# Two of six lower parts by an accumulating transfer in place of a GpSimd subtraction (attention and gated layer, one core)

## The chip, the cores and the metric

One core of a Trainium2 chip runs the whole program. The metric is the device time of one execution in microseconds (us), the median of several runs. A separate profiled execution gives the trace.

## What is computed

`x` has shape 4 x 12480 x 128 and `inducing` 32 x 128; `w_in` is 128 x 2048, `w_out` 2048 x 128. For each of the four batches, with `s = 1/sqrt(128)`:

```
mab(q, kv) = softmax(s * q @ kv.T) @ kv
h = mab(inducing, x)           # 32 x 128: summary of the batch
y = mab(x, h)                  # 12480 x 128
u = y @ w_in                   # 12480 x 2048
g = u        where u >= 1
    0        where u <= -1
    (u+1)^2/4  between
out = g @ w_out                # 12480 x 128
```

## The kernel before, in words

The tokens of a batch stand in 26 chunks of 480, 104 chunks in all. Per batch, `summarize` makes `h` and multiplies it with `w_in` (tile `hw`, held as an upper and a lower fp32r part); `attend` makes the softmax weights of four chunks at a time (tile `aT`). Then `chunk` does the wide layer for 480 tokens. This part fills most of the time.

`chunk` walks over 8 pairs `k` of 128 hidden features each (NP = 8, 256 features a pair). For each pair: two hidden matmuls on TensorE into two PSUM banks (L953, "h"); on ScalarE `max(u+1, 0)` from PSUM into the tile `w` (L961, "r", one instruction for both banks where these lie side by side, 128 x 960, else two of 128 x 480), then the square over four (L947, "s"); on VectorE the bound, `min(max(u, 1), w)` (L966, "t"), which makes `w` the gated value `g`. The product with `w_out` is accumulated in one PSUM bank over all pairs (L1053), read as 8 pairs of two 128-feature halves, then transposed on VectorE (L1065, tile `oT`) and stored.

An fp32 matmul (tile `w` with weight `w_f`, pairs 2 and 5, "pf") takes TensorE much longer than an fp32r one. So six of the eight pairs (`SPLIT = (0, 1, 3, 4, 6, 7)`; the last chunk uses `END`) are split: an upper part `hi` of fp32r ("hi": on VectorE at L1024, ScalarE at L1021 or GpSimd at L1019, as the planner chooses), and a lower part `lo = w - hi` by a subtraction on GpSimd (L1027, "lo"). With the weight's own parts `w_hi` and `w_lo` there are three fp32r matmuls for each half: `w_lo` x `hi` and `w_hi` x `hi` ("p"), and `w_hi` x `lo` ("pl").

The order is set before anything runs. Every operation goes to a planner (`Plan`) with its engine or choice of engines, a cost, a lag until its result can be used, and a due time from the table `DUE` (ns, by kind and pair). `Plan.order` walks through planned time, takes for each engine the operation that is due first among those that are ready, assigns the buffers (`SLOTS`: 8 for `w`, 4 for `hi`, 4 for `lo`, 7 PSUM banks for the hidden values) and fixes the order in which each engine gets its instructions. Each engine's queue then runs strictly in that order and waits by semaphores. DMAs are issued on SyncE (SP), two each on ScalarE at the start and the end, and none on GpSimd.

`load_out` loads a pair's part of `w_out` (8-byte floats), joins it to fp32 and makes `w_f` or `w_hi` and `w_lo` once, during the first 62 us.

Of the kernel before, what the change touches and what calls it, by code (L numbers as in the profile page):

```python
# [9 lines left out]
F32 = mybir.dt.float32  # L10
F32R = mybir.dt.float32r
# [9 lines left out]

KEPT = {}

SLOTS = dict(
    h=7, o=1, xn=9, xT=26, xr=2, e1=1, eN=1, hw=6, hx=1, hy=1, w=8, hi=4, lo=4, aT=3, s2=2, a=1, ahi=1, oT=1
)
# [4 lines left out]


DUE = {
# [17 lines left out]
    "end": [-102350],  # L51
# [15 lines left out]
}  # L67

WARM = (28000, 180)
# [57 lines left out]
class Plan:  # L127
# [125 lines left out]
def attn_moe(  # L253
# [68 lines left out]
    def in_turn(pool, near=None):  # L322
        turns[pool] += 1
        return Slot(pool, turns[pool] - 1, near)
# [126 lines left out]
        joined = add(dict(DVE=(both, both + 130, due), POOL=(700, 850, due)), 0, 0, 0, join, [v], [mag, top])  # L451
        return joined, mag

    w_hi, w_lo, w_f, w_made = {}, {}, {}, {}
    in_made = []

    def load_in(j, when, due):
# [4 lines left out]
    def load_out(k, when, due):  # L462
        src = w_out[k * WS : (k + 1) * WS].rearrange("(p t) d -> p t d", t=2)
        whole, parted = any(k not in t for t in [SPLIT, END]), any(k in t for t in [SPLIT, END])
        by = lambda a: a.rearrange("p (t c) -> p t c", t=2)
        made, f = load_f32(src, when, due, after=got_all[0, 21])
        w_made[k] = []
        if whole:
            w_f[k] = const.tile([P, 2, C], F32, name=f"w_f{k}")
            w_made[k].append(add("ACT", 320, 450, due, lambda: nc.scalar.copy(w_f[k], by(f.tile)), [made], [f]))  # L470
        if not parted:
            return
        w_hi[k] = const.tile([P, 2, C], F32R, name=f"w_hi{k}")
        w_lo[k] = const.tile([P, 2, C], F32R, name=f"w_lo{k}")

        def lower():
            nc.gpsimd.tensor_sub(w_lo[k], by(f.tile), w_hi[k].bitcast(F32))

        made = add("ACT", 320, 450, due, lambda: nc.scalar.copy(w_hi[k], by(f.tile)), [made], [f])
        w_made[k].append(add("POOL", 650, 750, due, lower, [made], [f]))  # L480


    xT, xT_made, hT, hT_made, hw, hw_made = {}, {}, {}, {}, {}, {}
# [448 lines left out]
    def chunk(b, c):  # L932
# [4 lines left out]
        for k in range(NP):  # L937
# [39 lines left out]
            for i, h in enumerate(hs_):  # L977
                ts.append(add("DVE", 568, 700, at(due, "t", k) + i, ms[i], [s], [h, w]))
            plan.twins(*ts, 1070, 1200, LONE["t"])
            if kept:  # L980
                hi, lo = in_turn("hi"), in_turn("lo")
                for i, h in enumerate(hs_):
# [28 lines left out]
                    ([(w_hi, lo)], 218, "pl", ls, [lo]),  # L1011
                ]
            elif split:
                hi, lo = in_turn("hi"), in_turn("lo")

                def upper(hi=hi, w=w, by=[]):
                    engine = by[0].engine
                    if engine == "POOL":
                        nc.gpsimd.tensor_scalar(make(hi), w.tile, 1.0, 0.0, op0=ALU.mult, op1=ALU.add)  # L1019
                    elif engine == "ACT":  # L1020
                        nc.scalar.copy(make(hi), w.tile)  # L1021
                    else:

                        nc.vector.tensor_reduce(make(hi), w.tile.unsqueeze(3), axis=AX.X, op=ALU.max)  # L1024

                def lower(w=w, hi=hi, lo=lo):
                    nc.gpsimd.tensor_sub(make(lo), w.tile, hi.tile.bitcast(F32))  # L1027

                by = []
                ways = dict(  # L1030
                    DVE=(1061, 1285, at(due, "hi DVE", k)), ACT=(886, 1065, at(due, "hi ACT", k)),
                    POOL=(1000, 1180, at(due, "hi POOL", k)),
                )
                u = add(ways, 0, 0, 0, lambda upper=upper, by=by: upper(by=by), ts, [hi, w])
                by.append(u)
                l = add("POOL", 2236, 2340, at(due, "lo", k), lower, [u], [lo, w, hi])

                parts = [
                    ([(w_lo, hi), (w_hi, hi)], 436, "p", [u], [hi]),
                    ([(w_hi, lo)], 218, "pl", [l], [lo]),  # L1040
                ]
            else:
                parts = [([(w_f, w)], 806, "pf", ts, [w])]
            for terms, cost, kind, needs, uses in parts:
                for i in range(2):

                    def project(k=k, i=i, terms=terms):
                        for wt, g in terms:
                            first = acc.tile is None
                            if first:  # L1050
                                make(acc)
                            acc.parts -= 1
                            nc.tensor.matmul(  # L1053
                                acc.tile[:, :CW], wt[k][:, i, :], g.tile[:, i, :],
                                start=first, stop=(acc.parts == 0),
                            )

                    acc.parts += len(terms)
                    done.append(
                        add("PE", cost, cost + 200, at(due, kind, k) + i, project, [*needs, *w_made[k]], [*uses, acc])  # L1060
                    )


        def turn():
# [73 lines left out]
```

## Time and profile before

| what | before |
|---|---|
| median of 3 runs | 1733.42 us (1731.18 to 1733.91) |
| profiled execution: span | 1730.3 us |
| median less that span (what lies around the instructions, and the difference of executions) | 3.1 us |
| granted TensorE clock, mean | 0.999 |
| first output transpose / last | 93.9 us / 1725.1 us |
| HBM read / written | 48.94 MB / 25.56 MB |

The span goes from the first to the last instruction of the one profiled execution; its own time is the span and what lies around it, which the trace doesn't hold; the 3.1 us is the nearest to it that is known. PE is TensorE's matmuls, PEld its weight loads, DVE VectorE, ACT ScalarE, POOL GpSimd, SP the engine that issues DMAs. In a group's row stand line, engine, operation, what it writes and reads, the shapes and the count, then busy time in us and the mean length of one in ns, then the idle time of the engine just before them and what ended it. A row of waits gives a total in us, how many, and the longest.

### The profile page before, as it was taken

The numbers are of one execution on the slowest core, as the hardware profiler recorded it, in microseconds if no ns is written. First come the engines' busy times: TensorE is split into PE (matmuls) and PEld (weight loads), VectorE is DVE, ScalarE is ACT, GpSimd is POOL, SyncE is SP. The second block draws the span as 40 slices with busy tenths as digits, with TensorE's granted clock in tenths as the row PEclk, the third lists the DMA queues.
The fourth block names the chain that finished last, engine by engine and source line by source line (L and its number), as shares of the span: only waits on it lengthen the run. The fifth ranks groups of instructions, "written<-read, shape, count | busy, mean of one in ns | idle before, by whom it ended". The sixth has DMA issues, their size and how long they took to land.

```text
span 1730.3 us, 26049 instructions
## 1 busy us (share of the span) xinstructions
PE 1696.6 (98%) x8062; PEld 1229.5 (71%) x8062; DVE 1626.2 (94%) x2167; ACT 1664.2 (96%) x2486; POOL 1612.6 (93%) x875
## 2 busy tenths in 40 slices
PE   6999999999999999999999999999999999999998
PEld 5667777777767777777777777777777677777776
DVE  5799999999999999999999999999999999999997
ACT  5699999999999999999999999999999999999997
POOL 1599999999899999999999999999989999999997
PEclk9999999999999999999999999999999999999999
DMA  9443323333334233343143333232212111111111
GB/s 235 112 74 69 74 58 70 57 62 61 70 66 77 47 72 63 66 75 68 31 93 54 74 68 69 51 66 52 42 34 53 33 30 30 35 35 35 33 31 18
DMA packets 427950, 105.76 MB, mean 61 GB/s; under 512 B 370562, under 2 KB 421218, under 8 KB 427810
## 3 DMA queue, kind: packets, MB, share of 16 engines
q1 hardware_dynamic: 426722, 103.84, 30.5%
q8 instruction: 64, 1.05, 0.3%
q14 instruction: 76, 0.62, 0.1%
q10 hardware_dynamic: 1088, 0.25, 0.1%
HBM read 48.94 MB, written 25.56 MB: 43 GB/s over the span
## 4 chain that ended last, share of the span: by engine, by line
PE 62%; ACT 16%; DVE 11%; issue 5%; POOL 3%; DMA 2%; SPq 1%; DVEq 0%; ACTq 0%; POOLq 0%
PE banks L1053 43%; PE banks L953 14%; ACT w L961 8%; ACT w L947 6%; DVE w L966 6%; DVE hi L1024 3%; POOL lo L1027 2%; PE banks L611 1%; PE banks L765 1%; ACT hi L1021 1%; PE banks L554 1%; SPq L532 1%; DMA xr<-in_x 1%; DVE oT L1065 1%; PE banks L514 1%
## 5 line engine op out<-in xcount | busy, mean ns | idle before, releaser
L1027 POOL TENSOR_TENSOR lo<-w,hi 128x960 fp32r<-128x960 f32 x623 | 1395.9, 2271 | 40.3 <-DVE hi L1024 17.9
L966 DVE SCALAR_TENSOR_TENSOR w<-banks,w 128x480 f32<-128x480 f32 (+1 forms) x1200 | 960.6, 838 | 35.9 <-ACT w L947 30.7
L961 ACT ACTIVATE w<-banks 128x480 f32<-128x480 f32 (+1 forms) x1352 | 843.7, 700 | 15.0 <-PE banks L953 13.9
L947 ACT ACTIVATE w<-w 128x960 f32<-128x960 f32 x832 | 842.2, 1049 | 2.7
L953 PE MATMUL banks<-aT,hw 128*128 128x480 f32 x1664 | 605.6, 432 | 7.3 <-DVE w L966 5.2
L1053 PE MATMUL banks<-hi,w_lo 128*128 128x480 f32 x1246 | 492.0, 395 | 5.4 <-DVE oT L1065 3.3
L1024 DVE TENSOR_REDUCE hi<-w 128x960 fp32r<-128x960 f32 x409 | 464.7, 1142 | 18.2 <-PE banks L1053 1.2
L1053 PE MATMUL banks<-hi,w_hi 128*128 128x480 f32 x1246 | 472.9, 380 | 0.0
L953 PEld LDWEIGHTS banks<-aT,hw 128*128 128x128 f32 x1664 | 304.7, 188 | 167.6 <-DVE w L966 71.1
L1053 PE MATMUL banks<-w,w_f 128*128 128x480 f32 x836 | 391.4, 567 | 0.0
L1053 PE MATMUL banks<-lo,w_hi 128*128 128x480 f32 x1246 | 385.2, 395 | 0.8 <-POOL lo L1027 0.8
L1053 PEld LDWEIGHTS banks<-hi,w_lo 128*128 128x128 f32 x1246 | 234.2, 188 | 76.2 <-DVE oT L1065 18.0
L1053 PEld LDWEIGHTS banks<-lo,w_hi 128*128 128x128 f32 x1246 | 229.8, 188 | 76.2 <-POOL lo L1027 25.7
L1053 PEld LDWEIGHTS banks<-hi,w_hi 128*128 128x128 f32 x1246 | 234.2, 188 | 40.0 <-issue 7.2
L1053 PEld LDWEIGHTS banks<-w,w_f 128*128 128x128 f32 x836 | 155.9, 189 | 68.7 <-issue 50.9
L1019 POOL TENSOR_SCALAR hi<-w 128x960 fp32r<-128x960 f32 x140 | 139.6, 1002 | 19.3 <-DVE w L966 10.4
L1021 ACT CAST hi<-w 128x960 fp32r<-128x960 f32 x74 | 75.5, 1021 | 4.7 <-DVE w L966 3.1
L1065 DVE STREAM_TRANSPOSE oT<-banks 128x480 f32<-128x480 f32 x104 | 70.1, 674 | 7.9 <-PE banks L1053 6.5
L535 DVE STREAM_TRANSPOSE xT<-xr 128x480 f32<-128x480 f32 x78 | 51.2, 659 | 0.0
L808 POOL TENSOR_TENSOR a<-a,ahi 128x480 fp32r<-128x480 f32 (+1 forms) x28 | 34.5, 1232 | 0.6 <-ACT ahi L805 0.6
L441 POOL TENSOR_TENSOR w_in_sb<-hi,lo 128x256 f32<-128x256 f32 x8 | 6.1, 763 | 28.4 <-DVE hi L430 28.4
L611 PEld LDWEIGHTS banks<-xn,eN 120*32 120x32 f32 (+1 forms) x754 | 24.4, 109 | 11.1 <-ACT eN L603 4.4
(107 smaller groups left out, 580.0 us busy)
## 6 DMA issues: line engine op xcount, KB each, us to landing
out<-oT SPq DMA_DIRECT2D x414, 60.0 KB, 2.2
xn<-in_x SPq DMA_DIRECT2D x91, 240.0 KB, 4.2
xr<-in_x SPq DMA_DIRECT2D x312, 60.0 KB, 2.5
aT<-ahi SPq DMA_DIRECT2D x206, 60.0 KB, 2.0
aT<-a SPq DMA_DIRECT2D x206, 60.0 KB, 2.0
w<-in_moe_w_in SPq DMA_DIRECT2D x8, 256.0 KB, 5.7
w<-in_moe_w_out SPq DMA_DIRECT2D x8, 256.0 KB, 3.8
hw<-hy SPq DMA_DIRECT2D x32, 64.0 KB, 2.0
```

The source lines that it names most:

```text
L535: nc.vector.transpose(make(xT[b, c]), xr.tile.rearrange("c n i -> c (n i)"))
L611: nc.tensor.matmul(p[q * M : (q + 1) * M, :C], eN[g].tile[:, t, q * M : (q + 1) * M], xn[g * Q + q].tile[:, t, :], start=(t == 0), stop=(t ...
L947: nc.scalar.activation(w.tile, w.tile, AF.Square, scale=0.5)
L953: nc.tensor.matmul(make(h)[:, :CW], hw[b][ft // 4].tile[:, ft % 4 * P : (ft % 4 + 1) * P], aT[b, c].tile, start=True, stop=True,)
L961: each(of, i, hs_, lambda h, to: nc.scalar.activation(to, h, AF.Relu, bias=1.0), w)
L966: lambda h, t: nc.vector.scalar_tensor_tensor(h if kept else t, h, 1.0, t, op0=ALU.max, op1=ALU.min), w,
L1019: nc.gpsimd.tensor_scalar(make(hi), w.tile, 1.0, 0.0, op0=ALU.mult, op1=ALU.add)
L1021: nc.scalar.copy(make(hi), w.tile)
L1024: nc.vector.tensor_reduce(make(hi), w.tile.unsqueeze(3), axis=AX.X, op=ALU.max)
L1027: nc.gpsimd.tensor_sub(make(lo), w.tile, hi.tile.bitcast(F32))
L1053: nc.tensor.matmul(acc.tile[:, :CW], wt[k][:, i, :], g.tile[:, i, :], start=first, stop=(acc.parts == 0),)
L1065: nc.vector.transpose(make(oT).rearrange("c n i -> c (n i)"), acc.tile[:, :CW])
```

## The change

For pairs 1 and 4 (`SUMMED`) the upper part is written negated: `hi = -upper(w)`. The "p" matmuls take weights with their sign turned: `w_lo` is made as upper less whole, and a new tile `w_neg` (minus `w_hi`, one ScalarE instruction per pair at the start) stands for `w_hi`. When these four matmuls are done, a DMA issued on GpSimd (`accum_op=add`, L1065 of the new file) adds the tile `w` onto the tile `hi` inside SBUF, 128 x 960 elements, which leaves `w - upper(w)`, the lower part, in `hi`'s own buffer. The "pl" matmuls of that pair read it there. No `lo` buffer is taken. The planner's numbers for it are a cost of 1050 ns on GpSimd and a lag of 5500 ns. The other four split pairs are as before. The projections' loop becomes a function `project`, and the whole table `DUE` has other values, so the order changes everywhere (the first two pieces of the diff below the table are in `load_out`, the others in `chunk`); `SLOTS`, `SPLIT` and the other costs stay.

```
+SUMMED = (1, 4)
 DUE = {
-    "lo": [-32300, -100100, 33050, 7950, 14550, -101950, -18700, -9000],
+    "lo": [5160, -100970, -23640, -58290, -161850, -112180, 60810, 140260],
...
         def lower():
-            nc.gpsimd.tensor_sub(w_lo[k], by(f.tile), w_hi[k].bitcast(F32))
+            if k in SUMMED:
+                nc.gpsimd.tensor_sub(w_lo[k], w_hi[k].bitcast(F32), by(f.tile))
+            else:
+                nc.gpsimd.tensor_sub(w_lo[k], by(f.tile), w_hi[k].bitcast(F32))
...
+        if k in SUMMED:
+            w_neg[k] = const.tile([P, 2, C], F32R, name=f"w_neg{k}")
+            w_made[k].append(
+                add("ACT", 320, 450, due, lambda: nc.scalar.mul(w_neg[k], w_hi[k].bitcast(F32), -1.0), [made], [])
+            )
...
             elif split:
-                hi, lo = in_turn("hi"), in_turn("lo")
+                summed = k in SUMMED
+                hi = in_turn("hi")
+                lo = hi if summed else in_turn("lo")
+                sign = -1.0 if summed else 1.0
...
-                        nc.gpsimd.tensor_scalar(make(hi), w.tile, 1.0, 0.0, op0=ALU.mult, op1=ALU.add)
+                        nc.gpsimd.tensor_scalar(make(hi), w.tile, sign, 0.0, op0=ALU.mult, op1=ALU.add)
                     elif engine == "ACT":
-                        nc.scalar.copy(make(hi), w.tile)
+                        nc.scalar.activation(make(hi), w.tile, AF.Copy, scale=sign)
                     else:
-                        nc.vector.tensor_reduce(make(hi), w.tile.unsqueeze(3), axis=AX.X, op=ALU.max)
+                        nc.vector.tensor_reduce(
+                            make(hi), w.tile.unsqueeze(3), axis=AX.X, op=ALU.max, negate=summed or None
+                        )
...
-                    nc.gpsimd.tensor_sub(make(lo), w.tile, hi.tile.bitcast(F32))
+                    if summed:
+                        nc.gpsimd.dma_start(hi.tile, w.tile, accum_op=ALU.add)
+                    else:
+                        nc.gpsimd.tensor_sub(make(lo), w.tile, hi.tile.bitcast(F32))
...
-                l = add("POOL", 2236, 2340, at(due, "lo", k), lower, [u], [lo, w, hi])
+                if summed:
+                    l = add(
+                        "POOL", 1050, 5500, at(due, "lo", k), lower, project([(w_lo, hi), (w_neg, hi)], 436, "p", [u], [hi]),
+                        [w, hi],
+                    )
+                else:
+                    l = add("POOL", 2236, 2340, at(due, "lo", k), lower, [u], [lo, w, hi])
                 parts = [
                     ([(w_lo, hi), (w_hi, hi)], 436, "p", [u], [hi]),
                     ([(w_hi, lo)], 218, "pl", [l], [lo]),
                 ]
+                if summed:
+                    del parts[0]
```

The order on the engines shows it. In its rows the number behind a weight's name is the pair (`w_lo1` is pair 1), the numbers behind `hi`, `lo`, `w` tell the buffers apart, and the lines of after are its own (L963 for L953, L1000 for L1053, L1054 for L1019, L1065 and L1067 for L1027). TensorE before, in the middle of the program, a pair 1 and the beginning of pair 3:

```order
L1053 MATMUL banks_64<-hi_2487_8885,w_lo1_91 128x480
L1053 MATMUL banks_64<-hi_2487_8885,w_hi1_90 128x480
L1053 MATMUL banks_64<-hi_2487_8885,w_lo1_91 128x480
L1053 MATMUL banks_64<-hi_2487_8885,w_hi1_90 128x480
L1053 MATMUL banks_64<-lo_2498_8920,w_hi1_90 128x480 x2
L953 MATMUL banks_64<-aT_2408_8602,hw_1286_4743 128x480
L1053 MATMUL banks_64<-hi_2493_8912,w_lo3_94 128x480
```

The lower part's two matmuls stand right behind the upper part's four. TensorE after, near the same place, from a pair 4's upper part on:

```order
L1000 MATMUL banks_64<-hi_2269_8254,w_lo4_97 128x480
L1000 MATMUL banks_64<-hi_2269_8254,w_neg4_98 128x480
L1000 MATMUL banks_64<-hi_2269_8254,w_lo4_97 128x480
L1000 MATMUL banks_64<-hi_2269_8254,w_neg4_98 128x480
L1000 MATMUL banks_64<-w_2245_8180,w_f2_93 128x480 x2
L963 MATMUL banks_64<-aT_2181_7949,hw_1225_4624 128x480 x2
L963 MATMUL banks_64<-aT_2181_7949,hw_1234_4645 128x480 x2
L1000 MATMUL banks_64<-lo_2268_8248,w_hi3_94 128x480 x2
```

and the end of the same stretch, four rows on:

```order
L1000 MATMUL banks_64<-hi_2257_8221,w_hi1_90 128x480 x2
L963 MATMUL banks_64<-aT_2181_7949,hw_1234_4645 128x480 x2
L963 MATMUL banks_64<-aT_2181_7949,hw_1295_4865 128x480
L1000 MATMUL banks_64<-hi_2284_8317,w_lo7_104 128x480
L1000 MATMUL banks_64<-hi_2284_8317,w_hi7_103 128x480
L1000 MATMUL banks_64<-hi_2284_8317,w_lo7_104 128x480
L1000 MATMUL banks_64<-hi_2284_8317,w_hi7_103 128x480
L1000 MATMUL banks_64<-hi_2269_8254,w_hi4_96 128x480
```

Between the last matmul with `w_neg4` and the first that reads the summed `hi_2269_8254` now stand 2 fp32 and 19 fp32r matmuls of other pairs. GpSimd before, the middle of the program:

```order
L1027 TENSOR_TENSOR lo_2489_8901<-w_2467_8813,hi_2482_8857 128x960
L1027 TENSOR_TENSOR lo_2498_8920<-w_2472_8833,hi_2487_8885 128x960
L808 TENSOR_TENSOR a_2490_8904<-a_2490_8904,ahi_2491_8909 128x480
L1027 TENSOR_TENSOR lo_2508_8957<-w_2481_8855,hi_2493_8912 128x960
L1027 TENSOR_TENSOR lo_2515_8980<-w_2488_8895,hi_2506_8942 128x960
L1027 TENSOR_TENSOR lo_2521_9003<-w_2503_8934,hi_2516_8985 128x960
L1019 TENSOR_SCALAR hi_2530_9028<-w_2512_8974 128x960
```

and after:

```order
L1054 TENSOR_SCALAR hi_2396_8711<-w_2376_8646 128x960
L818 TENSOR_TENSOR a_2386_8681<-a_2386_8681,ahi_2390_8701 128x480
L1054 TENSOR_SCALAR hi_2402_8736<-w_2385_8677 128x960
L1065 DMA hi_2396_8711<-w_2376_8646 128x960
L1067 TENSOR_TENSOR lo_2408_8759<-w_2385_8677,hi_2402_8736 128x960
L1065 DMA hi_2403_8742<-w_2389_8696 128x960
L1067 TENSOR_TENSOR lo_2418_8792<-w_2400_8728,hi_2413_8780 128x960
L1054 TENSOR_SCALAR hi_2425_8817<-w_2411_8767 128x960
```

Two subtractions of six have become issues, with subtractions of other pairs queued behind them, and more upper parts stand on GpSimd. Over the program GpSimd goes from 623 subtractions to 415 and 208 transfers, and from 140 upper parts to 216; VectorE from 409 upper parts to 370, its bounds from 464 wide and 736 narrow to 637 and 390; ScalarE from 74 upper parts to 37, its rises from 312 wide and 1040 narrow to 358 and 948.

More of the change, by code (lines that the diff above doesn't have):

```diff
@@ L33 @@
 DUE = {
[17 rows of a table removed]
-    "end": [-102350],
[15 rows of a table removed]
[17 rows of a table added]
+    "end": [-197940],
[15 rows of a table added]
 }
@@ L452, in load_f32 @@
         return joined, mag
-    w_hi, w_lo, w_f, w_made = {}, {}, {}, {}
+    w_hi, w_lo, w_f, w_neg, w_made = {}, {}, {}, {}, {}
     in_made = []
@@ L979, in chunk, with project, terms_of @@
             plan.twins(*ts, 1070, 1200, LONE["t"])
+            def project(terms, cost, kind, needs, uses, k=k, due=due):
+                made = []
+                for i in range(2):
+                    def terms_of(i=i):
+                        for wt, g in terms:
+                            first = acc.tile is None
+                            if first:
+                                make(acc)
+                            acc.parts -= 1
+                            nc.tensor.matmul(
+                                acc.tile[:, :CW], wt[k][:, i, :], g.tile[:, i, :],
+                                start=first, stop=(acc.parts == 0),
+                            )
+                    acc.parts += len(terms)
+                    made.append(
+                        add("PE", cost, cost + 200, at(due, kind, k) + i, terms_of, [*needs, *w_made[k]], [*uses, acc])
+                    )
+                done.extend(made)
+                return made
             if kept:
@@ L1013, in chunk, with upper, lower @@
             elif split:
-                hi, lo = in_turn("hi"), in_turn("lo")
-                def upper(hi=hi, w=w, by=[]):
+                summed = k in SUMMED
+                hi = in_turn("hi")
+                lo = hi if summed else in_turn("lo")
+                sign = -1.0 if summed else 1.0
+                def upper(hi=hi, w=w, by=[], summed=summed, sign=sign):
                     engine = by[0].engine
                     if engine == "POOL":
-                        nc.gpsimd.tensor_scalar(make(hi), w.tile, 1.0, 0.0, op0=ALU.mult, op1=ALU.add)
+                        nc.gpsimd.tensor_scalar(make(hi), w.tile, sign, 0.0, op0=ALU.mult, op1=ALU.add)
                     elif engine == "ACT":
-                        nc.scalar.copy(make(hi), w.tile)
+                        nc.scalar.activation(make(hi), w.tile, AF.Copy, scale=sign)
                     else:
-                        nc.vector.tensor_reduce(make(hi), w.tile.unsqueeze(3), axis=AX.X, op=ALU.max)
-                def lower(w=w, hi=hi, lo=lo):
-                    nc.gpsimd.tensor_sub(make(lo), w.tile, hi.tile.bitcast(F32))
+                        nc.vector.tensor_reduce(
+                            make(hi), w.tile.unsqueeze(3), axis=AX.X, op=ALU.max, negate=summed or None
+                        )
+                def lower(w=w, hi=hi, lo=lo, summed=summed):
+                    if summed:
+                        nc.gpsimd.dma_start(hi.tile, w.tile, accum_op=ALU.add)
+                    else:
+                        nc.gpsimd.tensor_sub(make(lo), w.tile, hi.tile.bitcast(F32))
                 by = []
@@ L1035, in chunk @@
                 by.append(u)
-                l = add("POOL", 2236, 2340, at(due, "lo", k), lower, [u], [lo, w, hi])
+                if summed:
+                    l = add(
+                        "POOL", 1050, 5500, at(due, "lo", k), lower, project([(w_lo, hi), (w_neg, hi)], 436, "p", [u], [hi]),
+                        [w, hi],
+                    )
+                else:
+                    l = add("POOL", 2236, 2340, at(due, "lo", k), lower, [u], [lo, w, hi])
                 parts = [
@@ L1041, in chunk @@
                 ]
+                if summed:
+                    del parts[0]
             else:
                 parts = [([(w_f, w)], 806, "pf", ts, [w])]
[L1044 to L1061, printed above, removed]
+            for part in parts:
+                project(*part)
         def turn():
```

62 rows, old and new, of the table DUE are left out of this document.

## Prediction

> **What bounds the kernel now.** I read the page's first part for the busy shares, then stretches of time, the spacing of TensorE's matmuls, its waits, and last the groups of instructions that the change touches.
>
> ```profile
> PE 1696.6 (98%) x8062; PEld 1229.5 (71%) x8062; DVE 1626.2 (94%) x2167; ACT 1664.2 (96%) x2486; POOL 1612.6 (93%) x875
> ```
> ```profile
> core 0: us, PE busy (x) PEld busy (x) DVE busy (x) ACT busy (x) POOL busy (x), PEclk, DMA share, GB/s
> 0.00:50.00 50.00, 35.93 (x440) 26.92 (x441) 27.72 (x87) 27.76 (x68) 9.80 (x19) 1.00 0.89 231
> 50.00:100.00 50.00, 46.09 (x325) 32.38 (x324) 40.75 (x80) 37.74 (x67) 32.80 (x27) 1.00 0.44 93
> 100.00:400.00 300.00, 297.53 (x1417) 215.27 (x1416) 288.03 (x365) 297.36 (x431) 291.17 (x156) 1.00 0.35 66
> ...
> 1200.00:1600.00 400.00, 396.77 (x1690) 287.62 (x1689) 387.19 (x494) 395.27 (x582) 387.38 (x203) 1.00 0.19 37
> ...
> 1700.00:1730.00 30.00, 25.00 (x96) 17.36 (x94) 19.42 (x25) 19.39 (x28) 21.11 (x11) 0.95 0.15 24
> ```
>
> From 100 us to 1700 us all four engines are nearly full at a granted clock of 1.00. A busy TensorE can hide stalls, so its pace comes from the starts in the timeline (start, length, then what ran):
>
> ```profile
> 1005.44 1.01 PE L554 MATMUL banks<-xT,indT 128*32 128x480 f32 x8
> 1006.38 1.15 PE L1053 MATMUL banks<-lo,w_hi 128*128 128x480 f32 x4
> ...
> 1018.57 1.08 PE L611 MATMUL banks<-xn,eN 120*32 120x128 f32 x32
> 1019.58 0.70 PE L953 MATMUL banks<-aT,hw 128*128 128x480 f32 x2
> ...
> 1716.76 0.38 PE L1053 MATMUL banks<-hi,w_hi 128*128 128x480 f32 x1
> 1716.98 0.60 PE L1053 MATMUL banks<-lo,w_hi 128*128 128x480 f32 x2
> 1717.42 1.77 PE L1053 MATMUL banks<-w,w_f 128*128 128x480 f32 x4
> 1718.66 0.75 PE L1053 MATMUL banks<-hi,w_lo 128*128 128x480 f32 x1
> 1719.25 0.37 PE L1053 MATMUL banks<-hi,w_hi 128*128 128x480 f32 x1
> ```
>
> A 480-wide fp32r matmul starts 0.218 us after the one before it (1716.98 to 1717.42 holds two). The two fp32 ones (four records) and one fp32r take 1719.25 - 1717.42 = 1.83 us, so one fp32 matmul is (1.83 - 0.218) / 2 = 0.806 us. Four scoring matmuls take 1006.38 - 1005.44 = 0.94 us. The program has 1664 hidden and 3738 split projections: 5402 x 0.218 = 1178; 418 fp32 projections x 0.806 = 337; 52 scoring groups x 0.94 = 49. For the other 1408 records (transposes, weighted sums, warm-up) I put 95 us, an estimate at 0.07 each, between the 0.03 of the weighted sums' records (32 in 1019.58 - 1018.57) and the 0.12 of the scoring's (8 in 0.94). The sum, 1659, leaves some 71 of 1730.3 us in which TensorE isn't at its pace. The first two rows above lack 18 us of busy time and the last 5, so some 45 us of stall are spread over the middle. That is the most that a better middle can give. What ended the weight loads' idle times (total, times, longest):
>
> ```profile
> PEld banks L953 <- DVE w L966: 71.1, 221, 1.7
> ...
> PEld banks L1053 <- POOL lo L1027: 26.9, 71, 0.9
> PEld banks L1053 <- DVE oT L1065: 18.0, 53, 1.4
> ```
>
> Part of these lies under running matmuls, but as shares they say: VectorE's bound at L966 first, GpSimd's lower part second.
>
> **The change, part by part.** The counts of after are from its order; the durations are from these groups (busy us, mean ns):
>
> ```profile
> L1027 POOL TENSOR_TENSOR lo<-w,hi 128x960 fp32r<-128x960 f32 x623 | 1395.9, 2271 | 40.3 <-DVE hi L1024 17.9 <-PE banks L1053 6.6 <-ACT w L947 3.4
> ...
> L961 ACT ACTIVATE w<-banks 128x480 f32<-128x480 f32 x1040 | 562.6, 606 | 14.6 <-PE banks L953 13.7
> L966 DVE SCALAR_TENSOR_TENSOR w<-banks,w 128x960 f32<-128x960 f32 x464 | 523.8, 1144 | 21.5 <-ACT w L947 17.1 <-PE banks L1053 2.0 <-issue 0.8
> ...
> L1024 DVE TENSOR_REDUCE hi<-w 128x960 fp32r<-128x960 f32 x409 | 464.7, 1142 | 18.2 <-PE banks L1053 1.2 <-POOL lo L1027 0.6
> L966 DVE SCALAR_TENSOR_TENSOR w<-banks,w 128x480 f32<-128x480 f32 x736 | 446.2, 645 | 14.4 <-ACT w L947 13.6
> ...
> L961 ACT ACTIVATE w<-banks 128x960 f32<-128x960 f32 x312 | 309.8, 1012 | 0.4 <-PE banks L953 0.2
> ...
> L1019 POOL TENSOR_SCALAR hi<-w 128x960 fp32r<-128x960 f32 x140 | 139.6, 1002 | 19.3 <-DVE w L966 10.4 <-ACT w L961 6.8 <-ACT eN L603 0.6
> L1021 ACT CAST hi<-w 128x960 fp32r<-128x960 f32 x74 | 75.5, 1021 | 4.7 <-DVE w L966 3.1 <-PE banks L1053 1.5
> ```
>
> *TensorE:* the number of projection matmuls is the same (in 416 the negated weight takes the upper weight's place): 0.
> *GpSimd:* 208 subtractions go, at 1395.9 / 623 = 2.24: -466. Upper parts go from 140 to 216: +76. 208 transfers are issued there. No row shows a GpSimd issue. The nearest are the queue's issue below, 0.59, and the subtraction, 2.27. I take 1.0, the single-input pass, as the lighter of the two kinds of GpSimd work: +208. Sum -182; by the ends -268 or +82.
> *VectorE:* upper parts 409 to 370: -44. More bounds become wide: +173 x 1.13 - 346 x 0.61 = -15. Sum -59. The negated reduction is costed as the plain one.
> *ScalarE:* upper parts 74 to 37: -38. Rises: 46 more wide (+46), 92 fewer narrow (-50). Sum -42. Two negated weights are made before the first chunks: under 1 us in all, beside loads; at most +1 if that cover is gone.
>
> So each of the three gains 42 to 182 us of room while TensorE keeps its 1659. Between no gain and 45 I take 15, one third: VectorE's busy time falls by only 4% and ScalarE's by 2.5%, and most of the stall ends on these, while GpSimd's share of the waits (26.9 of 116) is the one that the change cuts hard.
>
> *The new wait:* before, the lower part was made beside the upper part's matmuls. Now the transfer overwrites the upper part, so GpSimd waits for these matmuls (whatever is queued behind it waits too), and the last two projections wait for its landing; so do 205 rises on ScalarE, for the buffer w. Its price rests on the time from issue to landing:
>
> ```profile
> L831 SPq DMA_DIRECT2D aT<-a x206: 507/588/1759, 83.5 to 1673.0; - x103
> DMA to landing us min/median/max: 1.9/2.0/3.8
> ```
> ```profile
> q1 hardware_dynamic: 426722, 103.84, 30.5%
> ...
> xn<-in_x SPq DMA_DIRECT2D x91, 240.0 KB, 4.2
> ...
> aT<-a SPq DMA_DIRECT2D x206, 60.0 KB, 2.0
> ```
>
> In the first 50 us the engines moved 231 GB/s at a share of 0.89: 260 full. 480 KB then take 1.9 us, and 3.8 if the destination is read too. The 60 KB transfer inside SBUF lands in 2.0, of which 0.24 is its own bytes: 1.76 fixed. So 3.7 or 5.5, and 0.4 more if GpSimd's issue takes 1.0 rather than 0.59: from 4.1 to 5.9. By the two rows of 60 and 240 KB carried on in a line it would be 7.1; those 240 KB come from DRAM in short pieces, so I give it less weight. I take 5.0, the middle of 4.1 to 5.9. The share of the DMA engines rises from 30% by 208 x 1.9 / 1730 = 23% (46% if read twice), so they don't fill.
>
> By the page "DMA: Bandwidth & Descriptors" of the Trainium skill, section "Anatomy of one DMA — SWDGE (gpsimd) path", a DMA issued on GpSimd takes about 2.0 us plus its bytes at 436 GB/s. An estimate by it is 3.1 us, or 4.3 if the read counts twice, earlier than my 5.0; no run here shows such a transfer yet.
>
> In after's order TensorE has, between the end of the four matmuls and the first that needs the landing, work of 5.2 to 9.1 us at the paces above, median 6.3 over the 208. A landing after 5.0 (and 0.16 for the last matmul's end: 0.38 long, 0.218 spacing) stays under all of them: 0.
>
> Sum on the profiled execution: 1730.3 - 15 = 1715.3. The runs' median lies 3.1 above that span, so 1718.4, rounded 1718.
>
> **Rivals.** *Late landing (slower).* With T the time from issue to landing, a transfer costs TensorE what T + 0.16 exceeds its distance. Summed over the 208 distances: 13 us at T = 5.85, 26 at 6.05, 58 at 6.35, 127 at 6.85. It eats the gain from T = 5.9 on, which is the upper end above; at 6.35 the time is 1718 + 58 = 1776. For it: the double read, the line through 60 and 240 KB, and landings that spread to 3.8 over a median of 2.0. Against it: 5.0 leaves 0.9.
>
> *GpSimd doesn't get lighter.* From an issue of (466 - 76) / 208 = 1.88 us on it is as full as before, and the gain is gone: 1733. At 2.27 it is busy 1612.6 + 82 = 1694; if the idle time that it has now (1730 - 1613 = 117) stays, it sets the end at 1733 + 82 = 1815. The subtraction's narrow spread speaks against stretched work there:
>
> ```profile
> L1027 POOL TENSOR_TENSOR lo<-w,hi x623: 2226/2270/2347, 73.9 to 1719.7; 128x960 fp32r<-128x960 f32 x156
> ```
>
> The Trainium skill's page "SBUF — State Buffer", section "SBUF: two separate sides", has the rule that speaks for such an issue: a VectorE operation on both its ports keeps GpSimd from writing descriptors. The trace can't show it before there are any.
>
> *Nothing happens.* The stalls are those of a schedule where each thing is planned just in time; room on the other engines doesn't reach TensorE: 1731 to 1736.
>
> **How the numbers follow.** A measurement of this kernel tells about 0.2% (3.5 us) from no change. On time with a gain over 3.5 us: 0.63. Same: 0.13. Late landing 0.19 and heavy issue 0.05, both slower: 0.24. Likeliest alone: 1718, from 1700 to 1730. The range takes 1697 (36 of the 45 gained) below and 1770 (late landing up to T = 6.3) above; about 2 in 10 lie outside.
>
> **What would show it.** Right: GpSimd busy near 1430, its issues near 1.0 us, landings near 5, and waits of TensorE for the transfer of a few us in total. Wrong: landings at 6 or more with TensorE's first idle row naming the transfer; issues over 1.9 us; or TensorE's waits for VectorE's bound as long as before in spite of lighter engines. Tail and start should move by under 3 us.

## The result and the profile after

| | before | after |
|---|---|---|
| median of the runs side by side | 1732.70 us (1731.18 to 1733.91) | 1870.16 us (1867.26 to 1871.42) |
| ratio | 1 | 1.0788, 95% interval 1.0772 to 1.0803 |
| profiled execution: span | 1730.3 us | 1867.1 us |
| granted TensorE clock, mean | 0.999 | 0.976 |

Forecast were 1718 and 1697 to 1770; the kernel became 137 us slower. One execution of kernel 5 below ran 2798.6 us at a granted clock of 0.559 and is left out of that kernel's median. L976 of the new file is L966 of the old one, L963 is L953, L1000 is L1053, L812 is L802, L841 is L831.

The busy shares and two stretches of time, after:

```profile
PE 1747.7 (94%) x8056; PEld 1253.5 (67%) x8056; DVE 1592.7 (85%) x1953; ACT 1658.1 (89%) x2408; POOL 1413.7 (76%) x950
```
```profile
core 0: us, PE busy (x) PEld busy (x) DVE busy (x) ACT busy (x) POOL busy (x), PEclk, DMA share, GB/s
100.00:400.00 300.00, 283.52 (x1294) 203.24 (x1293) 262.66 (x308) 272.86 (x392) 234.30 (x155) 0.97 0.64 117
...
1200.00:1600.00 400.00, 381.65 (x1658) 273.93 (x1657) 350.96 (x414) 366.98 (x527) 315.69 (x210) 0.98 0.53 98
```

Every engine became idler at once: TensorE from 98% to 94% (with part of its work at a lower clock, see below), VectorE from 94% to 85%, ScalarE from 96% to 89%, GpSimd from 93% to 76%. No engine is the bound; they wait for something between them. What changed elsewhere in these rows is the share of the DMA engines, 0.35 to 0.64, and the clock, 1.00 to 0.97. The queues and the times from issue to landing (median us, last column):

```profile
q0 software_dynamic: 29952, 102.25, 30.0%
q1 hardware_dynamic: 426722, 103.84, 28.7%
...
hi<-w POOLq DMA_DIRECT2D x208, 480.0 KB, 5.5
...
xn<-in_x SPq DMA_DIRECT2D x91, 240.0 KB, 5.2
xr<-in_x SPq DMA_DIRECT2D x312, 60.0 KB, 2.9
aT<-ahi SPq DMA_DIRECT2D x206, 60.0 KB, 3.3
aT<-a SPq DMA_DIRECT2D x206, 60.0 KB, 4.6
```

The first row is new. The old transfers move the same bytes as before, but the one of tile `aT` that took 2.0 us takes 4.6, and `xn` 5.2 instead of 4.2. The waits, after (total us, times, longest):

```profile
ACT w L971 <- PE banks L963: 126.7, 133, 3.8
PEld banks L963 <- DVE w L976: 105.3, 168, 3.8
...
DVE a L812 <- DMA aT<-a: 64.5, 22, 5.1
...
PEld banks L1000 <- DMA hi<-w: 57.9, 66, 3.9
...
PE banks L963 <- DVE w L976: 45.8, 34, 3.4
...
PE banks L1000 <- DMA hi<-w: 31.7, 39, 3.5
```

Two of the large waits have a transfer behind them. TensorE waits for the summed lower part (last row, and the weight loads of the fourth): that is the wait that the change adds. VectorE waits 64.5 us, 22 times, at L812 for the transfer `aT<-a`. Before it waited 1.8 us, 3 times:

```profile
DVE a L802 <- DMA aT<-a: 1.8, 3, 0.8
```

Nothing in the diff touches that line: the tile `a` has one buffer for the weights of up to four chunks, two transfers to `aT` read it for each chunk, and the next transposition into it stands until the last of them has landed. Behind it in VectorE's strict queue stand the bounds of L976, and TensorE's hidden matmuls need the PSUM banks that these free. So it comes out as TensorE's wait for L976, with ScalarE behind that. The timeline around one of them (start, length, work, idle time before):

```profile
160.78 1.97 SPq L841 DMA_DIRECT2D aT<-a  x2
...
166.59 0.68 DVE L812 STREAM_TRANSPOSE a<-s 128x480 f32<-128x480 f32 x1 [4.35 <-DMA aT<-a]
167.20 1.11 DVE L1059 TENSOR_REDUCE hi<-w 128x960 fp32r<-128x960 f32 x1
168.23 2.21 DVE L976 SCALAR_TENSOR_TENSOR w<-banks,w 128x960 f32<-128x960 f32 x2
...
169.43 0.48 PE L963 MATMUL banks<-aT,hw 128*128 128x480 f32 x1 [2.76 <-DVE w L976]
```

The transfers issued from 160.8 on have landed at 166.6. VectorE idles for 4.35 us; the bounds that stood behind it come from 168.2 on, and TensorE idles 2.76 us until the first of them is through at 169.4. And one of the late lower parts:

```profile
594.21 0.89 POOL L1065 DMA_DIRECT2D hi<-w  x1 [0.98 <-PE banks L1000]
...
599.00 0.92 PE L963 MATMUL banks<-aT,hw 128*128 128x480 f32 x3
...
602.92 0.49 PE L1000 MATMUL banks<-hi,w_hi 128*128 128x480 f32 x1 [3.00 <-DMA hi<-w]
...
604.38 0.60 PE L1000 MATMUL banks<-hi,w_lo 128*128 128x480 f32 x1
604.78 0.60 PE L1000 MATMUL banks<-hi,w_hi 128*128 128x480 f32 x1
605.18 0.60 PE L1000 MATMUL banks<-hi,w_lo 128*128 128x480 f32 x1
```

The transfer issued at 594.2 was needed at 599.9 and had landed at 602.9, 8.7 us after its issue, beside four loads of `xn`. The last three rows show what comes on top: matmuls start 0.40 us apart, not 0.218. Stretches at these two places:

```profile
163.00:165.00 2.00, 1.94 (x8) 1.41 (x8) 0.00 (x0) 1.84 (x3) 1.92 (x2) 1.00 1.10 216
...
599.90:602.90 3.00, 0.02 (x1) 0.00 (x0) 0.92 (x2) 0.65 (x2) 2.23 (x2) 1.00 1.13 253
603.70:606.90 3.20, 3.20 (x10) 2.64 (x9) 3.02 (x4) 2.72 (x3) 1.69 (x1) 0.52 0.52 98
```

In both stalls the DMA engines are full (share 1.10 and 1.13; a packet counts whole where it starts, so a short stretch can pass 1), and behind the second the granted clock is 0.52. Cut into 500 slices of 3 us, the time from 100 to 1600 us has a DMA share over 0.9 in 32% of them; before it was 3%. The mean of 0.60 hides that.

### The profile page after: what moved, and what is told of

It is laid out like the page before. It is cut to its first block, busy times and chain, and to the rows that moved or that the text cites. A ratio compares the mean times of both kernels' runs of the same rounds, so it can differ in the third digit from the quotient of the medians.

```text
span 1867.1 us, 25857 instructions
## 1 busy us (share of the span) xinstructions
PE 1747.7 (94%) x8056; PEld 1253.5 (67%) x8056; DVE 1592.7 (85%) x1953; ACT 1658.1 (89%) x2408; POOL 1413.7 (76%) x950
## 3 DMA queue, kind: packets, MB, share of 16 engines
q0 software_dynamic: 29952, 102.25, 30.0%
q1 hardware_dynamic: 426722, 103.84, 28.7%
## 5 line engine op out<-in xcount | busy, mean ns | idle before, releaser
L1067 POOL TENSOR_TENSOR lo<-w,hi 128x960 fp32r<-128x960 f32 x415 | 962.1, 2362 | 74.9 <-PE banks L1000 36.3
L976 DVE SCALAR_TENSOR_TENSOR w<-banks,w 128x960 f32<-128x960 f32 (+1 forms) x1027 | 947.6, 954 | 55.3 <-ACT w L957 44.0
L963 PE MATMUL banks<-aT,hw 128*128 128x480 f32 x1664 | 575.0, 433 | 48.0 <-DVE w L976 45.8
L1000 PE MATMUL banks<-hi,w_lo 128*128 128x480 f32 x1246 | 490.7, 394 | 4.7 <-DVE hi L1059 1.6
L1000 PE MATMUL banks<-hi,w_hi 128*128 128x480 f32 x1246 | 450.4, 395 | 32.4 <-DMA hi<-w 31.7
L963 PEld LDWEIGHTS banks<-aT,hw 128*128 128x128 f32 x1664 | 311.4, 192 | 218.3 <-DVE w L976 105.3
L1059 DVE TENSOR_REDUCE hi<-w 128x960 fp32r<-128x960 f32 x370 | 423.3, 1145 | 40.0 <-PE banks L1000 23.2
L1000 PE MATMUL banks<-w,w_f 128*128 128x480 f32 x836 | 388.8, 574 | 0.0
L1054 POOL TENSOR_SCALAR hi<-w 128x960 fp32r<-128x960 f32 x216 | 221.8, 1036 | 128.8 <-DVE w L976 54.2
L1065 POOL DMA_DIRECT2D hi<-w x208 | 183.9, 885 | 169.2 <-PE banks L1000 54.7
L1000 PEld LDWEIGHTS banks<-hi,w_hi 128*128 128x128 f32 x1246 | 236.5, 193 | 94.8 <-DMA hi<-w 57.9
L1000 PEld LDWEIGHTS banks<-hi,w_lo 128*128 128x128 f32 x1246 | 239.0, 192 | 65.0 <-DVE oT L1097 12.7
L1000 PE MATMUL banks<-lo,w_hi 128*128 128x480 f32 x830 | 277.9, 410 | 0.9 <-POOL lo L1067 0.8
L1000 PEld LDWEIGHTS banks<-w,w_f 128*128 128x128 f32 x836 | 159.4, 192 | 78.8 <-issue 63.1
L1000 PEld LDWEIGHTS banks<-lo,w_hi 128*128 128x128 f32 x830 | 158.8, 193 | 52.7 <-issue 23.4
L1000 PE MATMUL banks<-hi,w_neg 128*128 128x480 f32 x416 | 158.8, 382 | 0.0
L1000 PEld LDWEIGHTS banks<-hi,w_neg 128*128 128x128 f32 x416 | 79.0, 190 | 12.7 <-issue 0.2
L812 DVE STREAM_TRANSPOSE a<-s 128x480 f32<-128x480 f32 (+1 forms) x28 | 18.9, 676 | 71.1 <-DMA aT<-a 64.5
```

The lines of the kernel that those rows point to most:

```text
L812: nc.vector.transpose(make(a)[:rows], s2.tile[:rows].rearrange("p n m -> p (n m)"))
L963: nc.tensor.matmul(make(h)[:, :CW], hw[b][ft // 4].tile[:, ft % 4 * P : (ft % 4 + 1) * P], aT[b, c].tile, start=True, stop=True,)
L976: lambda h, t: nc.vector.scalar_tensor_tensor(h if kept else t, h, 1.0, t, op0=ALU.max, op1=ALU.min), w,
L1000: nc.tensor.matmul(acc.tile[:, :CW], wt[k][:, i, :], g.tile[:, i, :], start=first, stop=(acc.parts == 0),)
L1054: nc.gpsimd.tensor_scalar(make(hi), w.tile, sign, 0.0, op0=ALU.mult, op1=ALU.add)
L1065: nc.gpsimd.dma_start(hi.tile, w.tile, accum_op=ALU.add)
```

## The experiments

Each kernel was run beside the kernel before; the medians of before lay between 1732.4 and 1733.6 us. Line numbers are each kernel's own (L1005 of kernel 1 is L1000 of after, L816 of kernel 3 is L812). "Full 3 us slices" is the part of those 500 slices with a share over 0.9, where it was counted.

| kernel | median us | ratio (95%) | `hi<-w` landing, median us | `aT<-a` landing, median us | full 3 us slices |
|---|---|---|---|---|---|
| before | 1732.7 | 1 | none | 2.0 | 3% |
| after | 1870.2 | 1.079 (1.077 to 1.080) | 5.5 | 4.6 | 32% |
| 1: two buffers | 1795.5 | 1.036 (1.035 to 1.038) | 5.5 | 4.6 | |
| 2: 32 columns summed | 1723.9 | 0.995 (0.9935 to 0.9965) | 2.4 | 2.0 | 3% |
| 3: no landing waited for | 1825.2 | 1.053 (1.0515 to 1.055) | 5.5 | 4.6 | |
| 4: plain copy | 1764.7 | 1.019 (1.017 to 1.020) | 3.6 | 2.9 | 14% |
| 5: 1 and 3 together | 1759.4 | 1.016 (1.014 to 1.017) | 5.5 | 4.5 | |
| 6: half the columns summed | 1747.6 | 1.009 (1.007 to 1.0105) | 3.8 | 2.9 | 15% |
| 7: two pairs, planned again | 1755.7 | 1.013 (1.011 to 1.014) | 5.6 | 4.7 | 36% |
| 8: one pair, planned again | 1727.9 | 0.997 (0.996 to 0.999) | 4.9 | 2.0 | 13% |
| 9: none, planned again | 1730.4 | 0.998 (0.9975 to 0.999) | none | 2.0 | |
| 10: 7 with 32 columns summed | 1719.4 | 0.992 (0.991 to 0.994) | 2.4 | 2.0 | |
| 11: 8 with 32 columns summed | 1716.0 | 0.990 (0.989 to 0.9915) | 2.3 | 2.0 | |
| 12: 7, no landing waited for | 1735.1 | 1.0015 (1.0006 to 1.0024) | 5.5 | 4.7 | |

**1. Two buffers for `a` and `ahi`.** Order and traffic stay.

```
+    made_of = dict(a=0, ahi=0)
...
+            made_of[slot.pool] += 1
+            side = f"_{made_of[slot.pool] % 2}"
...
-            shape or s, dtype or d, tag=f"{slot.pool}{slot.place}", ...
+            shape or s, dtype or d, tag=f"{slot.pool}{slot.place}{side}", ...
```

> After's order with two buffers in turn for the tiles a and ahi, so VectorE's transpose into a no longer waits for the last aT transfers that read it (64.5 us in 22 waits after, 1.8 before); traffic and the landing wait stay. Theory C (the transfers crowd out aT, and VectorE stands still on a): the 64.5 us go and with them about half of the 91 us at half clock (worth 22): near 1870 - 87 = 1783. Theory L (TensorE waits for the landing): within 10 us of 1870.

1795.5 us: 75 less than after. The wait at L812 for `aT<-a` is gone, the mean clock is back at 0.995, and of the two large waits for a transfer the landing's is left:

```profile
PEld banks L1005 <- DMA hi<-w: 64.7, 74, 3.2
...
PE banks L1005 <- DMA hi<-w: 36.2, 43, 2.8
```

So the wait for tile `a`, which the prediction didn't have, is worth half of the loss. (`ahi` has two buffers here too, but in after no wait stands on it; kernel 5 doubles `a` alone.)

**2. Hardly any bytes.** All instructions, semaphores and waits stay; the transfer has 32 of 960 columns.

```
-    nc.gpsimd.dma_start(hi.tile, w.tile, accum_op=ALU.add)
+    nc.gpsimd.dma_start(hi.tile[:, 0, :32], w.tile[:, 0, :32], accum_op=ALU.add)
```

> After's order, but each of the 208 accumulating transfers adds only 32 of 960 columns; the other columns of the lower part are left wrong. Issue, waits and order stay, the bytes go. L and C both: landing near 2.2 us, no waits for it, aT back at 2.0, clock 0.999, and the time that my sum forecast, 1718, or 1733 if room on the other engines doesn't reach TensorE. Rival O (the new order or the issue on GpSimd is what costs): above 1780.

1723.9 us, 8.5 faster than before beside it. A stretch of it, and its transfers:

```profile
400.00:800.00 400.00, 398.74 (x1870) 290.56 (x1870) 374.76 (x447) 390.43 (x565) 338.87 (x227) 1.00 0.38 67
```
```profile
L1065 POOL DMA_DIRECT2D hi<-w x208: 827/877/1201, 83.2 to 1709.9; - x104
...
DMA to landing us min/median/max: 2.0/2.4/6.1
```

TensorE is busy 398.7 of 400 us with GpSimd at 339, and the issue costs GpSimd 0.877 us as with all the bytes (0.881). So the whole 146 us between this kernel and after come with the bytes; the issues, the longer order and the chain of semaphores cost nothing that shows. Nor do the bytes slow the engines' own work by much: in after and in this kernel the wide bound on VectorE takes 1145 and 1146 ns in the mean, the upper part there 1145 and 1145, the subtraction on GpSimd 2362 and 2299, which is 15 us of busy time on an engine that idles for 453.

**3. No matmul waits for a landing.** The last two projections of pairs 1 and 4 read a tile of zeros, all traffic stays.

```
-    acc.tile[:, :CW], wt[k][:, i, :], g.tile[:, i, :],
+    acc.tile[:, :CW], wt[k][:, i, :],
+    (still if kind == "pl" and k in SUMMED else g.tile)[:, i, :],
```

> After's order and full traffic, but the last two projections of pairs 1 and 4 read a constant tile of zeros, so TensorE never waits for a landing; the lower parts of these pairs are left out of the sum. L: the 90 us of waits for the transfer and half of the low clock go: 1780 to 1800. C: 1850 or more, since aT and a are as slow as after.

1825.2 us: 45 less than after, between the two theories. What stays is VectorE's wait, not smaller than in after:

```profile
DVE a L816 <- DMA aT<-a: 68.9, 23, 4.6
```

The late landing, the rival of the prediction, is a real cost, but under a third of the 146, and less than the wait for `a`.

**4. A plain copy of the same bytes.**

```
-    nc.gpsimd.dma_start(hi.tile, w.tile, accum_op=ALU.add)
+    nc.gpsimd.dma_start(hi.tile, w.tile)
```

> After's order with a plain copy of w onto hi in place of the accumulation: as many bytes written, issue and waits as after, no read of the destination; the lower part is left wrong. If the second read makes the landing late: landing 3.7 to 4.2 us and the time between 1720 and 1790. If the size alone does: landing within 0.4 of 5.5 and the time within 20 us of 1870.

1764.7 us, as the first of the two expectations has it. What the accumulation itself adds is seen in the same rows of this kernel:

```profile
L1065 POOL DMA_DIRECT2D hi<-w x208: 530/607/753, 82.6 to 1750.7; - x104
...
DMA to landing us min/median/max: 2.8/3.6/9.4
```
```profile
q0 software_dynamic: 29952, 102.25, 17.7%
```

Issue 0.61 us against 0.88, landing 3.6 against 5.5, and 17.7% of the engines' time against 30.0% for the same 102.25 MB: 1.5 us against 2.7 of all 16 engines for each transfer (the share times the span, 1763.1 and 1867.1, over 208). Without the accumulation 105 of the 146 us are gone. Whether a second read of the destination is what it adds, no run shows.

**5. Both waits away.** Two buffers for `a` (not for `ahi`), and a zeros tile as in 3; all traffic stays.

> Both remedies together, full traffic: two buffers in turn for a, and the last two projections of pairs 1 and 4 read a tile of zeros, so nothing on TensorE waits for a landing; their lower parts are left out of the sum. If a's hold (75 us by the first run) and the landing wait (45 by the third) are all that the bytes cost, this comes to the time without the bytes, 1724, within 10. If the traffic also delays other things (the next chunk's buffers w and hi, the loads of x), it stays above 1745.

1759.4 us: 110.7 of the 146.3 are gone, which is near the 75 + 45 of the two alone. 35.6 stay with neither wait there, so the traffic also delays other things. In its trace VectorE waits 19.4 us in 13 times for `xr`, up to 4.2 (kernel 2: 2.7 us), ScalarE waits 5.2 for the transfers that read `w`, and 17 us ahead of the tail are at half the clock, which is up to 8.5 us. These may be most of the 35.6, but no run takes them away one by one, so the shares aren't shown.

**6. Half the bytes.** One of the tile's two halves is summed.

```
-    nc.gpsimd.dma_start(hi.tile, w.tile, accum_op=ALU.add)
+    nc.gpsimd.dma_start(hi.tile[:, 0, :], w.tile[:, 0, :], accum_op=ALU.add)
```

> After's order with the accumulation of one half of each tile only (480 of 960 columns, 240 KB in place of 480); the other half's lower part is left wrong. Landing by a line between 2.1 us (32 columns) and 5.2: 3.7. If each transfer costs by its bytes, the time is half way between 1724 and 1870: 1797. If it costs only where landings pass what the order leaves (5.2 us and more on TensorE, 2.7 planned for aT), it is much nearer to 1724: below 1760.

1747.6 us. The first half of the bytes costs 24 us, the second 123: it isn't a price per byte, and the second expectation (below 1760) holds. The landing is 3.8 us, under the planned 5.5; TensorE waits 5.4 us for it, and VectorE 19.1 for `aT<-a`, which has 2.9. The plain copy takes nearly the same share of the engines (17.7 and 17.4%): in both 14 to 15% of the slices are full, and the loss on kernel 2 is 24 us here and 41 there.

**7, 8, 9. Planned again with what was measured.** The table `DUE` was searched anew, with the planner told: in 7 a lag of 6.7 us for the sum (5.5 in after), 5.0 for `aT` (2.7), 5.5 for `xr` (3.2), 7.0 for `xn` (3.0), an issue of 0.9, and `a=2` in `SLOTS`; in 8 one pair only, with lags of 5.9, 4.7, 5.0 and 6.5 and one buffer; 9 is the control, no pair summed, the numbers and buffers of before.

```
-SUMMED = (1, 4)
+SUMMED = (4,)          # 8;  () in 9
...
-    "POOL", 1050, 5500, at(due, "lo", k), lower, ...
+    "POOL", 900, 6700, at(due, "lo", k), lower, ...      # 7;  900, 5900 in 8
```

> Both pairs summed by transfers of full size, all of the reference computed, but planned with the landings that the trace of after shows: 6.7 us for the sum in place of 5.5, 5.0 for aT in place of 2.7, 5.5 for xr (3.2), 7.0 for xn (3.0), 0.9 for the issue (1.05), two buffers for a, and the table of due times searched anew for these lags. If the loss was a plan that believed in early landings, TensorE's waits for the transfer fall below 15 us, the clock is back at 0.999, and the time is near that without the bytes, 1724, within 10. If the bytes cost in ways that a plan can't cover (the 37 us left when both waits were gone), it stays above 1740.

> The same for pair 4 alone (half of the transfers, 104), planned with 5.9 us for the sum, 4.7 for aT, 5.0 for xr, 6.5 for xn, one buffer a, due times searched anew. GpSimd is relieved by half as much. If bytes cost in proportion beyond the plan's reach, it beats the two-pair version by about half of that one's distance to 1724; if the room on GpSimd is what gains, it is the slower of the two by some 4 us; before 1732 is passed either way if the lags are the whole cause.

> Control for the two: no pair summed (all six by subtraction, as before), before's lags and buffers, due times searched anew by the same search. What it gains over before is the search's and not the transfers': between 1725 and 1735 if before's table was near its best; if it comes below 1720, the gain of the two others says nothing about transfers.

Seven: 1755.7 us. It is 114 below after, yet 23 above before, so the second theory holds. Its chain and its waits:

```profile
PE 67%; DMA 14%; DVE 6%; ACT 5%; POOL 3%; issue 3%; SPq 1%; DVEq 0%; ACTq 0%; POOLq 0%
```
```profile
PEld banks L1000 <- DMA hi<-w: 30.1, 30, 2.1
...
PE banks L1000 <- DMA hi<-w: 17.1, 18, 1.6
```

The plan holds 6.7 us for a sum, and of the 208 a quarter take over 7.1 (up to 8.5). The planner knows a transfer only as a lag, not as something that fills the engines, and 36% of the slices are full. That transfers placed close together lengthen each other is a reading of this; no run spreads them out. Eight: 1727.9 us, faster than before by 0.26% (0.13 to 0.40) and the one version with transfers and the whole computation that beats before. It beats seven by 28 us, more than the half of seven's distance to 1724 (16) that bytes in proportion would give. Nine: 1730.4, within its 1725 to 1735. Of the 5 us that 8 gains, the control gains 2.6 without any transfer. The other 2.5 are not clear of noise: the intervals of 8 and 9 share 0.9975 to 0.9987.

**10 and 11. The same orders without the bytes.** Kernels 7 and 8 with the 32 columns of kernel 2.

> The order, lags and buffers of the kernel that was planned again with the measured landings for two pairs (1755.7 us), with the accumulating transfer cut to 32 of 960 columns: nearly all the bytes are gone, every instruction and wait stays where it was (the lower parts are wrong). Theory A, the bytes still cost what the plan can't hold, because a quarter of the sums land after 7.1 us where 6.7 was planned: without them the order gives about 1722 to 1730, so some 25 to 35 us of the 1755.7 are the bytes'. Theory B, the order itself is poor, since a plan with long lags leaves little freedom: the time stays at 1745 to 1756. In between: both share it.

> The kernel that was planned again for one pair alone (1727.9 us), with its accumulating transfers cut to 32 of 960 columns in the same order (the lower part of that pair is wrong). Theory A, at one pair the bytes fit beside the other transfers once the plan knows the landings (waits for a landing are about 10 us in its trace, those of TensorE itself 4 us): the time falls by no more than 4 us, to 1724 to 1728. Theory B, the bytes still cost time spread over small waits: it falls to 1715 to 1722, and the whole gain of the lighter GpSimd shows.

1719.4 and 1716.0 us; for 10 theory A holds, with a little more than its 25 to 35 us. So the bytes still cost 36 us in 7 and 12 us in 8, although the plan held longer landings. The chain of kernel 10 beside that of 7:

```profile
PE 87%; ACT 6%; DVE 3%; issue 2%; POOL 1%; DMA 1%; SPq 0%; DVEq 0%; ACTq 0%; POOLq 0%
```

DMA falls from 14% to 1%, TensorE rises from 67% to 87%. Against the control of 1730.4 the orders without the bytes gain 11 us with two pairs and 14 with one; the bytes take back all of it and more in the first case, most of it in the second. Each of the three has a table of its own, so these gains are of the lighter engines and of the search together; as one pair gains no less than two, they can't simply be put down to room on GpSimd. For 11 the second theory holds: 12 us stood in waits that its parent's trace shows as 4 us of TensorE and 7 of its weight loads.

**12. Planned again, and no landing waited for.** Kernel 7, in which the last two projections of both pairs read a tile of weights (the upper weights of pairs 0 and 1, put into one tile).

```
-    acc.tile[:, :CW], wt[k][:, i, :], g.tile[:, i, :],
+    acc.tile[:, :CW], wt[k][:, i, :],
+    first_two.rearrange("p t c -> p (t c)")[:, :CW]
+    if kind == "pl" and k in SUMMED else g.tile[:, i, :],
```

> The kernel planned again for two pairs (1755.7 us), same order and all its bytes, but the last two projections of pairs 1 and 4 read a tile of weights that stands there since the start, in place of the landed lower part (the lower parts of these pairs are left out of the output). So no matmul waits for a landing. With nearly all bytes gone the same order took 1719.4 us: 36.4 us are to be explained. Theory A, the landing wait alone (in the trace TensorE waits 17.1 us for landings in 18 gaps over 0.5 us, its weight loads 30.1 us): most of the 36 us go, 1720 to 1730. Theory B, the slower transfers of the others (the mean landing of tile aT's halves doubled) and small waits through VectorE and GpSimd: under 15 us go, 1741 or more. In between: shared, in proportion.

1735.1 us: 20.7 of the 36.4 go, 15.7 stay. Shared, as between the two theories. The rest comes without a wait of TensorE for a landing. In its trace VectorE waits 8.3 us for `xr` and 5.1 for sums that hold a `hi` buffer, ScalarE 6.1 for sums that hold a `w` buffer; which part of the 15.7 each has isn't shown.

## Why the prediction was wrong, step by step

- *TensorE's work is the same: right.* 8056 records against 8062, and without the bytes it is busy 398.7 of 400 us. (1408 records at 0.07 us are 98.6 us, not 95; the stall left in the middle is then 45 us, as the prediction has it.)
- *GpSimd gets lighter: right.* Forecast busy 1430 with issues of 1.0 us; measured 1413.7, and 0.881 (838 to 1198). The rival of a heavy issue falls.
- *The gain of 15 us from room on the other engines: the sign right, the size too high, and only once the bytes are gone.* With the bytes gone after's order gains 8.5 us on before. That orders searched again gain 14.2 and 17.5 (1733.57 of before beside them, less 1719.37 and 1716.03) is near 15 partly by luck: the control's new search gains 2.6 by itself.
- *Landing 5.0 us, one value: a size was off.* Measured were 4.4 at the least, 5.5 in the median, a quarter over 6.0, and 9.2 at the most. It goes with what else is in flight (an overlap of over 0.5 us counted): in the trace the median is 4.9 for the 9 that flew nearly alone, 5.2 beside `aT`, 5.9 for the 92 behind another sum, 6.7 beside `xn`. The Trainium skill's page "DMA: Bandwidth & Descriptors", section "Anatomy of one DMA — SWDGE (gpsimd) path", gave 3.1 or 4.3 by estimate; the plain copy with 2.8 to 3.6 agrees with the former, the sum with 5.5 lies above both, and the measurement decides. The landings above the median bring the waits: 57.9 us of weight loads and 31.7 of matmuls, worth 45 us by kernel 3, between the 26 and 58 that the rival "late landing" has for 6.05 and 6.35. A term was left out too: the issue starts 0.54 us (median; 0.30 to 3.24) after the last of the four matmuls ends, so with 5.5 and 0.16 the median transfer already needs 6.2 of the 6.3 us that the order leaves.
- *"The share of the DMA engines rises from 30% by 208 x 1.9 / 1730 = 23% (46% if read twice), so they don't fill": this step failed.* The share itself came out between the two: 30.0%, beside 28.7% for the old transfers. The conclusion was drawn from an average over the span. In slices of 3 us the engines are full a third of the time, and the old transfers land later: the halves of `aT` in 1.99 us (median of the 19 with no sum in flight between issue and landing) or in 4.3 (of the 393 beside one). The Trainium skill's page "DMA: Bandwidth & Descriptors", section "Queues, rings and completion order", says that an engine takes a whole packet from one ring before it turns to the next; the landings agree with such a queueing, though no run here separates packets from plain lack of room. The prediction put the delay of the old transfers at nothing, and named no buffer that they hold. The tile `a` was the one on which VectorE stood still: 2.7 us planned, 4.6 taken in the median, 64.5 us of waits, worth 75 us by kernel 1. One of its signs of being wrong came from this: the weight loads' wait for VectorE's bound rose from 71.1 to 105.3 us.
- *The clock: not in the prediction.* A mean clock of 0.976 over 1867 us is up to 45 us lost. The records show it at 0.5 in 19 windows of 3.4 or 6.8 us ahead of the tail, 89 us in all; 18 stand at a TensorE gap of 1.8 to 3.8 us, one at two gaps of 0.8. The Trainium skill's page "TensorE: Matmul & The Clock Gate", Part 1, describes this: after an idle window of about 3.4 us the clock goes to half. The trace agrees on the window (3.413 us) and the half, but less idling was enough. The 19 start on one grid of 3.413 us, and TensorE idled for 0.515 to 0.89 of the grid step before each; in no other step at full clock (from 80 us to 20 us before the end) was it idle for more than 0.40. In kernel 1 the clock is 0.995, so up to 36 of its 75 us came back through the clock. A stall that lowers the clock can cost 1.7 us more for each 3.4 us at half.

Taken together: 146.3 us with the bytes, of which 110.7 go when the two waits are removed, and 35.6 lie in traffic beyond them. That the loss comes from the bytes is shown (2, 10, 11); that it goes through tile `a` and the landing is shown (1, 3, 5); which small waits make up the last 35.6 stays open.

## What to carry to other kernels

Cost a new transfer by what it does to the transfers that are already there: look at the DMA share in slices as short as a landing, not over the span, and at which buffer each old transfer holds and how much slack its planned time has. Full slices alone don't give the price: 32% of them went with 146 us in after, 36% with 36 us in kernel 7, whose plan left more room. An accumulating transfer inside SBUF took 1.8 times the engine time and 1.5 times the landing of a plain copy of the same bytes, so a subtraction that it saves must be worth more than that room. In a plan that knows transfers as lags alone, the kernel with one pair summed came out 0.26% faster than before, about half of which a new search gives without any transfer, and the one with two pairs 1.3% slower.

## What the runs showed of the hardware that was not expected

- The issue of such a transfer costs GpSimd the same for 32 columns as for 960 (0.877 and 0.881 us), and less without the accumulation (0.607).
- SyncE's issues became slower too: in after an issue of `aT<-a` takes 783 ns in the median and 2905 at the most, where it was 588 and 1759:

```profile
L841 SPq DMA_DIRECT2D aT<-a x206: 507/783/2905, 84.1 to 1809.9; - x103
```

- Not the length of one gap but the idle share of a fixed grid step goes with the half clock, in which 480-wide matmuls start 0.40 us apart instead of 0.218. In the 14 traces, in the same stretch of each, 46 of 47 drops came after a 3.413 us step of which TensorE idled for more than half (0.508 at the least), and one after 0.43. Steps idle for up to 0.46 stayed at full clock, even around a gap of 2.8 us (one each in kernels 1 and 3).
